# Linear attention and top-1 experts on one core: in three projection tiles the key maximum stands behind the reciprocal, the next tile's statistics behind the query feature, the value sum behind the rows' low part

## Chip, cores and metric

The kernel runs on one core of a Trainium2 chip (trn2). The metric is device time in microseconds of one execution, here the median of 3 runs.

## What is computed

A pre-norm block of two parts over 2048 tokens of width 512, in float32. The first part is linear attention with 32 heads of 16 (a learned feature map of two softmaxes per head); the second sends each token to one of 8 experts (top 1).

```python
def _A_ref(x, wqkv, w_phi, wo):
    H = 32; Dh = D // H
    qkv = (lambda x, *d: x.transpose(*d))((x @ wqkv).reshape(B, S, 3, H, Dh), 2, 0, 3, 1, 4)
    q, k, v = qkv[0], qkv[1], qkv[2]
    pq = jnp.einsum("bhsd,hdf->bhsf", q, w_phi)
    pk = jnp.einsum("bhsd,hdf->bhsf", k, w_phi)
    phi_q = jnp.concatenate([_softmax(pq, axis=-1), _softmax(-pq, axis=-1)], axis=-1)
    phi_k = jnp.concatenate([_softmax(pk, axis=-1), _softmax(-pk, axis=-1)], axis=-1)
    kv = jnp.einsum("bhsf,bhsd->bhfd", phi_k, v)
    z  = jnp.einsum("bhsf->bhf", phi_k)
    num = jnp.einsum("bhqf,bhfd->bhqd", phi_q, kv)
    den = jnp.einsum("bhqf,bhf->bhq", phi_q, z)[..., None] + 1e-6
    ...
h = x + _A_ref(_layernorm(x, axis=-1), A_wqkv, A_w_phi, A_wo)
h2 = h + _B_ref(_layernorm(h, axis=-1), B_w_gate, B_w1, B_w2)
```

## The kernel before

**Stages.** The tokens are cut into 16 tiles of 128 rows (`NT`). A first stage (the projection tiles) walks over them, projects each to keys, values and queries, builds the features and adds up the state. A second stage multiplies the query features by the state, projects out and ranks the experts. The rest runs the experts' two matrices over groups of tokens. Every float32 product is made of three matmuls on a high and a low part (`mm3`, L89): high by high, high by low, low by high, where the first factor is loaded as the weights. The low part is the number less its high part.

**A projection tile c** (the loop at L826). TensorE runs the key projection `pk` of tile c (12 matmuls of 512 columns), the value projection `pv` of tile c+1 (24 of 260 columns, L671), the query projection `pq` of tile c (12 of 512), then the state products `kvps` of tile c-1 (L708) and the 8 transposes `ptq` of the query feature of tile c-1 (L717). In the projections the rows' parts `xh` and `xl` are the weights that are loaded; in a value projection the third matmul is the first to need `xl`.

**The features** (`feat1`, `feat1b`, `feat2`, L643 to L668). VectorE takes minimum `mn` and maximum `mx` of each head from PSUM and writes `t`, the differences to both; ScalarE takes the exponential of `t`, scaled by `rstd`; VectorE sums it (`sm`, L661) and takes the reciprocal (L662); GpSimd (POOL) multiplies, which gives the feature `ph` (L664). In tile c this is done for the query of tile c-1 (`feat2` at L831) and for the key of tile c, then the query of tile c is begun.

**Statistics** (`s_lna`, L612). The mean and variance of the rows of tile c+2: ScalarE's sum (L616), POOL's `xmv` (L617, L620), ScalarE's square (L619), then POOL's `xve` and `rstd` (L622, L623). They are written in tile c and run on into tile c+1. **Values** (`s_v`, `s_ve`, `s_vf`): ScalarE copies `pv` of tile c+1 to `v`, scaled by `rstd` (L682), copies the gate columns `xwg` (L684) and makes `vt` from a row and `rm` = mean times `rstd` (POOL, L693; ScalarE, L697); POOL adds `vt` to `v` (L702). **Rows** (`s_x`, L626): ScalarE rounds the transposed rows of tile c+2 to `xh` (L84 in `hi_of`), POOL writes `xl` (L634). `xh` and `xl` have two buffers and wait for the query projection that reads the old ones.

**What sets the order.** The Tile framework places the instructions of each engine in one row at build time, by the code's order and its own estimates; `with after(i)` (L147) keeps the instructions within it behind `i`. On the chip each instruction waits, by semaphores, for the results and buffers that it needs. `pin` holds the instructions that others are kept behind: `pin["f2"]` is the last feature's multiplication, `pin["rc"]` the last reciprocal, `pin["ex"]` the last exponential.

Of the kernel before, what the change touches and what calls it, by code (L numbers as in the profile page):

```python
# [16 lines left out]
OP = mybir.AluOpType  # L17
AX = mybir.AxisListType
# [31 lines left out]
VC = 4 * (DH + 1)  # L50
KW = 32
LNA = 1


@with_exitstack
def kernel(
# [14 lines left out]
    V, A, G, T = nc.vector, nc.scalar, nc.gpsimd, nc.tensor  # L71
# [73 lines left out]
    pin = {}  # L145

    def after(i):  # L147
        return tc.issue_after(i.ins) if i is not None else ExitStack()
# [266 lines left out]
    with ExitStack() as actx:  # L415
# [40 lines left out]
        st = [dict() for _ in range(NT)]  # L456
# [79 lines left out]
        if True:  # L536
# [75 lines left out]
            def s_lna(c):  # L612
                xt, sm, mv = st[c]["xt"], work.tile([P, 2], F32, name="xsum", bufs=4), work.tile([P, 2], F32, name="xmv", bufs=4)
                jk = wp.tile([P, D], BF16, name="jk", bufs=2)
                with after(pin.get("pq")):
                    A.activation(jk, xt, AF.Copy, accum_out=sm[:, 0:1])  # L616
                G.tensor_scalar(mv[:, 1:2], sm[:, 0:1], -1.0 / D, None, op0=OP.mult)  # L617
                with after(pin["ex"]):
                    st[c]["sq"] = A.activation(jk, xt, AF.Square, bias=mv[:, 1:2], accum_out=sm[:, 1:2])  # L619
                G.tensor_scalar(mv[:, 0:1], sm[:, 0:1], 1.0 / D, None, op0=OP.mult)  # L620
                ve, rstd = work.tile([P, 1], F32, name="xve"), work.tile([P, 1], F32, name="rstd", bufs=4)
                G.tensor_scalar(ve, sm[:, 1:2], 1.0 / D, EPS, op0=OP.mult, op1=OP.add)  # L622
                G.tensor_tensor(rstd, ve, nhalf, op=OP.pow)  # L623
                st[c]["mean"], st[c]["rstd"] = mv[:, 0:1], rstd

            def s_x(c, eng=G):  # L626
                v = st[c]["xT"].rearrange("p (k t) -> p k t", k=KD)
                if c < NT - 1:
                    xh, xl = [work.tile([P, KD, P], F32R, name=n) for n in ("xh", "xl")]
                else:  # L630
                    xh, xl = [wp.tile([P, KD, P], F32R, name=n) for n in ("xhe", "xle")]
                st[c]["xi"] = hi_of(xh, v)
                st[c]["x"] = xh, xl
                return eng.tensor_tensor(xl, v, xh.bitcast(F32), op=OP.subtract)  # L634

            def split_o(t):
                v = slice(0, D // 2)
                r = wo_raw[t // 2][:, t % 2, :].rearrange("p (i d) -> p i d", i=2)
                with after(st[t + 5]["v"]):
                    hi_of(wohi[:, t, :, v], r)  # L640
                return lambda: G.tensor_tensor(wolo[:, t, :, v], r, wohi[:, t, :, v].bitcast(F32), op=OP.subtract)

            def feat1(p, c, whole=True):  # L643
                pv = p.rearrange("p (h f) -> p h f", f=DH)
                mn = work.tile([P, H], F32, name="mn")
                V.tensor_reduce(mn, pv, AX.X, OP.min)
                t = wp.tile([P, H, 2, DH], F32, name="t", bufs=3)
                V.tensor_tensor(t[:, :, 1, :], bc(mn, DH), pv, op=OP.subtract)
                return feat1b(p, c, t) if whole else t

            def feat1b(p, c, t):
                pv = p.rearrange("p (h f) -> p h f", f=DH)
                mx = work.tile([P, H], F32, name="mx")
                V.tensor_reduce(mx, pv, AX.X, OP.max)
                pin["f1"] = V.tensor_tensor(t[:, :, 0, :], pv, bc(mx, DH), op=OP.subtract)  # L655
                pin["ex"] = A.activation(t, t, AF.Exp, scale=st[c]["rstd"])  # L656
                return t.rearrange("p h s f -> p (h s) f")

            def feat2(t, tail=None):
                sm = work.tile([P, 2 * H], F32, name="sm")  # L660
                V.tensor_reduce(sm, t, AX.X, OP.add)  # L661
                pin["rc"] = V.reciprocal(sm, sm)  # L662
                ph = work.tile([P, NB * ROW], F32, name="ph", tag="ph", bufs=3)[:, 0:HF]
                pin["f2"] = G.tensor_tensor(ph.rearrange("p (a f) -> p a f", f=DH), t, bc(sm, DH), op=OP.mult)  # L664
                if tail:
                    with after(pin["f2"]):
                        tail()
                return ph  # L668
# [3 lines left out]
            def s_v(c):  # L672
                with after(pin["pj"]):
                    p, m, pw = proj2(st[c]["x"], wvhi, wvlo, "pv")
                s_ve(c, p, pw)
                s_vf(c)
                return m

            def s_ve(c, p, pw=None):
                v = v17[c % 3].rearrange("p (i h) f -> p i h f", i=2)[:, :, :, 0:DH]  # L680
# [10 lines left out]
            def s_vf(c, eng=None):  # L691
                rm = work.tile([P, 1], F32, name="rm")
                G.tensor_tensor(rm, st[c]["mean"], st[c]["rstd"], op=OP.mult)  # L693
                vt, v = row("vt", 2, "pc"), v17[c % 3][:, :, 0:DH]
                if eng is None:
                    with after(st[c]["v"] if c < 5 else None):
                        A.activation(vt, csv, AF.Copy, scale=rm)  # L697
                else:
                    eng.tensor_scalar(vt, csv, rm, None, op0=OP.mult)
                def add():  # L700
                    with after(pin["f2"]):
                        G.tensor_tensor(v, v, vt.rearrange("p (h f) -> p h f", f=DH), op=OP.add)  # L702

                if c > 1:
                    add()
                return add

# [51 lines left out]
            with after(warmup(6)):  # L759
                pc = bank("pcs")  # L760
                m = T.matmul(pc[:, 0:E], onesf, gsum, start=True, stop=True)
# [21 lines left out]
            with after(m):  # L783
                p0, m, _ = proj2(st[0]["x"], wvhi, wvlo, "pv", True)
# [41 lines left out]
            for c in range(NT - 1):  # L826
# [2 lines left out]
                    s_qt(0)  # L829
                if 0 < c < NT - 2:  # L830
                    st[c - 1]["fq"] = feat2(st[c - 1]["tq"])  # L831
                lo_o = split_o(c - 5) if 5 <= c < 9 else None
                tk = feat1(pk, c)
                if c == 0:
                    pf = [bank("pf") if dt < 2 else pss.tile([P, 512], F32, name="pf", tag="s") for dt in range(KD)]
                    for dt in range(KD):
                        fold_half(wq_raw, pf[dt], dt, 0)
                        fold_half(wq_raw, pf[dt], dt, 1)
                        fold_split(pf[dt], dt, wqhi, wqlo)
                    kvps.append(pss.tile([P, NG, 64], F32, name="kvps", tag="s")[:, :, 0:(DH + 1) * KW // 32])  # L840
                elif c < NT - 2:
                    vm = s_v(c + 1)
                if c in (3, 4):
                    pg = bank("pog")
                    fold_gate(pg, 2 * c - 6)
# [16 lines left out]
                else:  # L862
# [11 lines left out]
                        pq = proj(st[c]["x"], wqhi, wqlo, "pq")  # L874
                    if c + 2 < NT - 1:
                        with after(pin["f2"] if c == 1 else None):
                            s_x(c + 2)
                    st[c]["fk"] = feat2(tk, lo_o)
                    if c < NT - 3:
                        st[c]["tq"] = feat1(pq, c)  # L880
# [793 lines left out]
```

## Time and profile before

| | us |
|---|---|
| median of 3 runs (lowest to highest) | 633.94 (633.76 to 634.34) |
| the profiled execution | 633.68 |
| its span, from the first to the last instruction | 632.0 |
| TensorE busy in the span | 622.7 |

The profile is of one execution. Its time is 1.7 us longer than its span, for what lies around the first and last instruction. Busy times are of instructions on an engine; two that follow each other on one engine overlap by up to 0.1 us. Projection tile 8 begins at 98.85 us, tile 11 ends at 140.22 us.

### The profile page before, as it was taken

Reading aid. Unit: us, or ns where it says so; the run is one execution under the profiler, and the core shown is the slowest. Engines: PE = TensorE matmul, PEld = TensorE weight load, DVE = VectorE, ACT = ScalarE, POOL = GpSimd, SP = SyncE. Lnnn points to the kernel's source line nnn. Section 1 sums busy time; section 2 is a strip of 40 time slices with the busy share of each in tenths; the row PEclk is TensorE's granted clock in tenths of the full one; section 3 lists DMA queues with packets and bytes.
Section 4 is the critical chain, followed back from the end, with each engine's and each line's share of the span. In section 5 each row is a group of like instructions: output and inputs, shape, how many; then the busy total and the mean of one; then the engine's idle time right before and its main releaser. Section 6 shows DMA issues by size and latency. Waiting matters only on the chain. (4 is left out here: it accounts for less than half of the span.)

```text
span 632.0 us, 14731 instructions
## 1 busy us (share of the span) xinstructions
PE 622.7 (99%) x5455; PEld 555.6 (88%) x5455; DVE 452.8 (72%) x900; ACT 373.5 (59%) x673; POOL 247.5 (39%) x345
## 2 busy tenths in 40 slices
PE   9999999999999999999999999999999999999996
PEld 8888888888889999868998898989999889988884
DVE  7988786888898789965325666666556775579992
ACT  6666767577434439634325666566456666668781
POOL 5586788787616555621122221120301420023120
PEclk9999999999999999999999999999999999999999
DMA  8712111111002359249121485563755585569921
GB/s 319 250 36 66 37 51 52 51 52 35 18 20 85 118 204 380 100 158 419 48 69 52 164 307 204 199 235 135 272 170 208 186 335 164 195 222 374 415 81 36
DMA packets 25689, 103.09 MB, mean 163 GB/s; under 512 B 3422, under 2 KB 3422, under 8 KB 17536
## 3 DMA queue, kind: packets, MB, share of 16 engines
q1 hardware_dynamic: 21088, 88.15, 39.1%
q0 software_dynamic: 4368, 13.82, 6.5%
q8 instruction: 46, 0.75, 0.5%
q14 instruction: 43, 0.35, 0.2%
q10 hardware_dynamic: 144, 0.02, 0.0%
HBM read 93.56 MB, written 8.81 MB: 162 GB/s over the span
## 5 line engine op out<-in xcount | busy, mean ns | idle before, releaser
L235 DVE TENSOR_TENSOR wlo<-raw,whi 128x1024 fp32r<-128x1024 f32 (+1 forms) x133 | 151.9, 1165 | 27.3 <-ACT whi L84 25.6
L84 ACT ACTIVATE whi<-raw 128x1024 fp32r<-128x1024 f32 (+1 forms) x134 | 129.3, 998 | 1.6 <-DVE wlo L235 0.6
L168 POOL DMA_INDIRECT xg<-hbuf,gidx x34 | 42.9, 1261 | 132.6 <-DMA out_dram<-xg,sidx 33.3
L87 DVE TENSOR_TENSOR hA<-hs,hA 128x256 fp32r<-128x256 f32 (+1 forms) x84 | 36.6, 436 | 74.9 <-ACT hA L84 53.9
L664 POOL TENSOR_TENSOR ph<-t,sm 128x1024 f32<-128x1024 f32 x32 | 62.1, 1942 | 16.8 <-DVE sm L662 16.5
L90 PE MATMUL gw<-xhi,whi 128*128 128x256 f32 x224 | 64.1, 286 | 0.0
L92 PE MATMUL gw<-xhi,wlo 128*128 128x256 f32 x224 | 63.0, 281 | 0.0
L91 PE MATMUL gw<-xlo,whi 128*128 128x256 f32 x224 | 63.0, 281 | 0.0
L1423 ACT ACTIVATE hs<-gw 128x256 f32<-128x256 f32 x56 | 21.4, 383 | 63.2 <-PE gw L92 52.8
L661 DVE TENSOR_REDUCE sm<-t 128x64 f32<-128x1024 f32 x32 | 38.9, 1215 | 20.0 <-ACT t L656 17.9
L656 ACT ACTIVATE t<-t,rstd 128x1024 f32<-128x1024 f32 x32 | 36.8, 1151 | 27.2 <-DVE t L655 24.7
L181 POOL DMA_INDIRECT out_dram<-xg,sidx x17 | 19.9, 1169 | 79.4 <-DVE xg L1275 44.1
L90 PEld LDWEIGHTS gw<-xhi,whi 128*128 128x128 f32 x224 | 42.2, 188 | 1.7
L91 PEld LDWEIGHTS gw<-xlo,whi 128*128 128x128 f32 x224 | 42.3, 189 | 1.6
L92 PEld LDWEIGHTS gw<-xhi,wlo 128*128 128x128 f32 x224 | 42.2, 188 | 0.0
L90 PE MATMUL po<-wohi,xh 128*128 128x260 f32 x128 | 37.4, 293 | 0.0
L84 ACT ACTIVATE hA<-hs 128x256 fp32r<-128x256 f32 (+1 forms) x84 | 35.8, 427 | 2.6
L92 PE MATMUL po<-wohi,xl 128*128 128x260 f32 x128 | 36.5, 286 | 0.1
L91 PE MATMUL po<-wolo,xh 128*128 128x260 f32 x128 | 36.1, 282 | 0.0
L90 PE MATMUL pv<-wvhi,xh 128*128 128x260 f32 x120 | 34.3, 286 | 0.0
L92 PE MATMUL pv<-wvhi,xl 128*128 128x260 f32 x120 | 33.9, 283 | 0.0
L91 PE MATMUL pv<-wvlo,xh 128*128 128x260 f32 x120 | 33.9, 282 | 0.0
(425 smaller groups left out, 1922.9 us busy)
## 6 DMA issues: line engine op xcount, KB each, us to landing
raw<-in_w_dram SPq DMA_DIRECT2D x63, 1024.0 KB, 5.8
xt<-in_x_dram SPq DMA_DIRECT2D x32, 256.0 KB, 2.7
hbuf<-hb SPq DMA_DIRECT2D x8, 515.0 KB, 3.5
xT<-in_xTs_dram SPq DMA_DIRECT2D x16, 256.0 KB, 2.7
phT<-in_wv_dram SPq DMA_DIRECT2D x4, 256.0 KB, 3.6
phT<-in_wqkT_dram SPq DMA_DIRECT2D x4, 256.0 KB, 5.3
phT<-in_wqkT_dram SPq DMA_DIRECT2D x2, 512.0 KB, 6.1
phT<-in_wo_dram SPq DMA_DIRECT2D x2, 512.0 KB, 7.7
```

Source lines behind the costliest of these rows:

```text
L84: return A.activation(dst, src, AF.Copy)
L87: return V.tensor_tensor(dst, src, hi.bitcast(F32), op=OP.subtract)
L90: T.matmul(ps, ahi, bhi, start=first, stop=False)
L91: T.matmul(ps, ahi, blo, start=False, stop=False)
L92: return T.matmul(ps, alo, bhi, start=False, stop=last)
L168: G.indirect_dma_start(out=dst[0:n, :], out_offset=None, in_=hbuf if col else hbuf[0:S // 2, :], in_offset=bass.IndirectOffsetOnAxis(ap=gi ...
L181: m = G.indirect_dma_start(out=out, out_offset=bass.IndirectOffsetOnAxis(ap=sidx[0:n, col:col + 1], axis=0), in_=src[0:n, 0:D], in_offset= ...
L235: return eng.tensor_tensor(lo, r, h.bitcast(F32), op=OP.subtract)
L656: pin["ex"] = A.activation(t, t, AF.Exp, scale=st[c]["rstd"])
L661: V.tensor_reduce(sm, t, AX.X, OP.add)
L664: pin["f2"] = G.tensor_tensor(ph.rearrange("p (a f) -> p a f", f=DH), t, bc(sm, DH), op=OP.mult)
L1423: A.activation(h, p, AF.Silu)
```

## The change

In the tiles of `GL` (c = 8, 9, 10) three things are placed elsewhere; what is computed is the same. The key's maximum `mx` is kept behind the reciprocal of the query's sums (`pin["rc"]`). The last steps of the statistics of tile c+1, `xve` and `rstd`, are a function of their own (`s_lnb`) and kept behind the query feature's multiplication (`pin["f2"]`). The value sum (`add`) is kept behind `xl` of tile c+2.

```diff
--- before.py
+++ after.py
@@ -50,6 +50,7 @@
 VC = 4 * (DH + 1)
 KW = 32
 LNA = 1
+GL = range(8, 11)
 
 
 @with_exitstack
@@ -618,6 +619,12 @@
                 with after(pin["ex"]):
                     st[c]["sq"] = A.activation(jk, xt, AF.Square, bias=mv[:, 1:2], accum_out=sm[:, 1:2])
                 G.tensor_scalar(mv[:, 0:1], sm[:, 0:1], 1.0 / D, None, op0=OP.mult)
+                st[c]["ms"] = mv, sm
+                if c - 1 not in GL:
+                    s_lnb(c)
+
+            def s_lnb(c):
+                mv, sm = st[c]["ms"]
                 ve, rstd = work.tile([P, 1], F32, name="xve"), work.tile([P, 1], F32, name="rstd", bufs=4)
                 G.tensor_scalar(ve, sm[:, 1:2], 1.0 / D, EPS, op0=OP.mult, op1=OP.add)
                 G.tensor_tensor(rstd, ve, nhalf, op=OP.pow)
@@ -640,18 +647,19 @@
                     hi_of(wohi[:, t, :, v], r)
                 return lambda: G.tensor_tensor(wolo[:, t, :, v], r, wohi[:, t, :, v].bitcast(F32), op=OP.subtract)
 
-            def feat1(p, c, whole=True):
+            def feat1(p, c, whole=True, behind=None):
                 pv = p.rearrange("p (h f) -> p h f", f=DH)
                 mn = work.tile([P, H], F32, name="mn")
                 V.tensor_reduce(mn, pv, AX.X, OP.min)
                 t = wp.tile([P, H, 2, DH], F32, name="t", bufs=3)
                 V.tensor_tensor(t[:, :, 1, :], bc(mn, DH), pv, op=OP.subtract)
-                return feat1b(p, c, t) if whole else t
-
-            def feat1b(p, c, t):
+                return feat1b(p, c, t, behind) if whole else t
+
+            def feat1b(p, c, t, behind=None):
                 pv = p.rearrange("p (h f) -> p h f", f=DH)
                 mx = work.tile([P, H], F32, name="mx")
-                V.tensor_reduce(mx, pv, AX.X, OP.max)
+                with after(behind):
+                    V.tensor_reduce(mx, pv, AX.X, OP.max)
                 pin["f1"] = V.tensor_tensor(t[:, :, 0, :], pv, bc(mx, DH), op=OP.subtract)
                 pin["ex"] = A.activation(t, t, AF.Exp, scale=st[c]["rstd"])
                 return t.rearrange("p h s f -> p (h s) f")
@@ -673,8 +681,7 @@
                 with after(pin["pj"]):
                     p, m, pw = proj2(st[c]["x"], wvhi, wvlo, "pv")
                 s_ve(c, p, pw)
-                s_vf(c)
-                return m
+                return m, s_vf(c)
 
             def s_ve(c, p, pw=None):
                 v = v17[c % 3].rearrange("p (i h) f -> p i h f", i=2)[:, :, :, 0:DH]
@@ -697,11 +704,11 @@
                         A.activation(vt, csv, AF.Copy, scale=rm)
                 else:
                     eng.tensor_scalar(vt, csv, rm, None, op0=OP.mult)
-                def add():
-                    with after(pin["f2"]):
+                def add(behind=None):
+                    with after(pin["f2"]), after(behind):
                         G.tensor_tensor(v, v, vt.rearrange("p (h f) -> p h f", f=DH), op=OP.add)
 
-                if c > 1:
+                if c > 1 and c - 1 not in GL:
                     add()
                 return add
 
@@ -829,8 +836,11 @@
                     s_qt(0)
                 if 0 < c < NT - 2:
                     st[c - 1]["fq"] = feat2(st[c - 1]["tq"])
+                    if c in GL:
+                        with after(pin["f2"]):
+                            s_lnb(c + 1)
                 lo_o = split_o(c - 5) if 5 <= c < 9 else None
-                tk = feat1(pk, c)
+                tk = feat1(pk, c, True, pin["rc"] if c in GL else None)
                 if c == 0:
                     pf = [bank("pf") if dt < 2 else pss.tile([P, 512], F32, name="pf", tag="s") for dt in range(KD)]
                     for dt in range(KD):
@@ -839,7 +849,7 @@
                         fold_split(pf[dt], dt, wqhi, wqlo)
                     kvps.append(pss.tile([P, NG, 64], F32, name="kvps", tag="s")[:, :, 0:(DH + 1) * KW // 32])
                 elif c < NT - 2:
-                    vm = s_v(c + 1)
+                    vm, add = s_v(c + 1)
                 if c in (3, 4):
                     pg = bank("pog")
                     fold_gate(pg, 2 * c - 6)
@@ -874,7 +884,9 @@
                         pq = proj(st[c]["x"], wqhi, wqlo, "pq")
                     if c + 2 < NT - 1:
                         with after(pin["f2"] if c == 1 else None):
-                            s_x(c + 2)
+                            lx = s_x(c + 2)
+                        if c in GL:
+                            add(lx)
                     st[c]["fk"] = feat2(tk, lo_o)
                     if c < NT - 3:
                         st[c]["tq"] = feat1(pq, c)
```

In the rows below the numbers in the names are those of buffers; line numbers after the change are those of the changed file. On POOL, tile 8, before: the statistics of tile 9 (`xmv_1615`, `xve`, `rstd`), then `rm`, then the feature of tile 7's query (`ph_1641`), the value sum of tile 9 and the low part `xl` of tile 10's rows.

```order
L617 TENSOR_SCALAR xmv_1615<-xsum_1614 128x1
L620 TENSOR_SCALAR xmv_1615<-xsum_1614 128x1
L622 TENSOR_SCALAR xve_1621<-xsum_1614 128x1
L623 TENSOR_TENSOR rstd_1622<-xve_1621,fixed_66 128x1
L693 TENSOR_TENSOR rm_1679<-xmv_1615,rstd_1622 128x1
L664 TENSOR_TENSOR ph_1641<-t_1564,sm_1638 128x1024
L702 TENSOR_TENSOR v17_0_201<-v17_0_201,vt_1681 128x32x16
L634 TENSOR_TENSOR xl_1702<-xT_1537,xh_1701 128x512
```

The same place after:

```order
L618 TENSOR_SCALAR xmv_1615<-xsum_1614 128x1
L621 TENSOR_SCALAR xmv_1615<-xsum_1614 128x1
L672 TENSOR_TENSOR ph_1637<-t_1564,sm_1634 128x1024
L629 TENSOR_SCALAR xve_1639<-xsum_1614 128x1
L630 TENSOR_TENSOR rstd_1640<-xve_1639,fixed_66 128x1
L700 TENSOR_TENSOR rm_1679<-xmv_1615,rstd_1640 128x1
L641 TENSOR_TENSOR xl_1701<-xT_1537,xh_1700 128x512
L709 TENSOR_TENSOR v17_0_201<-v17_0_201,vt_1681 128x32x16
```

The query feature has moved ahead of `xve`, `rstd` and `rm`, and `xl` ahead of the value sum.

On ScalarE, tile 8, before: the statistics' square, `vt`, `v` and `xwg` of tile 9, the exponential of tile 8's key (`t_1646`), the high part `xh` of tile 10's rows.

```order
L619 ACTIVATE jk_1616,xsum_1614<-xt_1386,xmv_1615 128x512
L697 ACTIVATE vt_1681<-csv_204,rm_1679 128x512
L682 ACTIVATE v17_0_201<-pv_1652,rstd_1622 128x32x16
L684 ACTIVATE xwg_170<-pv_1652 128x8
L656 ACTIVATE t_1646<-t_1646,rstd_1473 128x1024
L84 ACTIVATE xh_1701<-xT_1537 128x512
```

And after:

```order
L620 ACTIVATE jk_1616,xsum_1614<-xt_1386,xmv_1615 128x512
L689 ACTIVATE v17_0_201<-pv_1652,rstd_1640 128x32x16
L664 ACTIVATE t_1646<-t_1646,rstd_1473 128x1024
L691 ACTIVATE xwg_170<-pv_1652 128x8
L704 ACTIVATE vt_1681<-csv_204,rm_1679 128x512
L85 ACTIVATE xh_1700<-xT_1537 128x512
```

`vt` has moved from ahead of `v` to behind the exponential and `xwg`; `v` now stands directly behind the square. `xh` is still behind all four.

On VectorE, tile 8, before: sum and reciprocal of tile 7's query (`sm_1638`), maximum and difference of tile 8's key, then the sum of the key's exponentials and the query of tile 8.

```order
L661 TENSOR_REDUCE sm_1638<-t_1564 128x64
L654 TENSOR_REDUCE mx_1648<-pk_1625 128x32
L662 RECIPROCAL sm_1638<-sm_1638 128x64
L655 TENSOR_TENSOR t_1646<-pk_1625,mx_1648 128x32x16
L661 TENSOR_REDUCE sm_1705<-t_1646 128x64
L646 TENSOR_REDUCE mn_1711<-pq_1688 128x32
```

And after:

```order
L669 TENSOR_REDUCE sm_1634<-t_1564 128x64
L670 RECIPROCAL sm_1634<-sm_1634 128x64
L662 TENSOR_REDUCE mx_1648<-pk_1621 128x32
L663 TENSOR_TENSOR t_1646<-pk_1621,mx_1648 128x32x16
L653 TENSOR_REDUCE mn_1711<-pq_1687 128x32
L669 TENSOR_REDUCE sm_1705<-t_1646 128x64
```

The reciprocal has moved ahead of the key's maximum, and the minimum of the query ahead of the sum of the key's exponentials. TensorE's row is the same before and after.

## Rows read from the trace of the kernel before

**Rows 1.** The page's span and first part: busy time, share of the span and number of instructions of each engine.

```profile
span 632.0 us, 14731 instructions
PE 622.7 (99%) x5455; PEld 555.6 (88%) x5455; DVE 452.8 (72%) x900; ACT 373.5 (59%) x673; POOL 247.5 (39%) x345
```

**Rows 2.** Whom TensorE waited for over the whole span: line waited at, releaser, us in total, times, longest us. The longest three.

```profile
PE warm L751 <- DVE onesf L419: 1.3, 1, 1.3
PE mh L90 <- PEq L1577: 0.6, 1, 0.6
PE ptq L722 <- POOL ph L664: 0.3, 1, 0.3
...
```

**Rows 3.** Windows of the projection tiles 8, 9, 10 and 11, each from the first matmul of its key projection `pk` to that of the next tile. Columns: window, its length, then busy us (and instructions) of PE, PEld, DVE, ACT and POOL, the granted clock, DMA share, GB/s.

```profile
98.85:109.37 10.52, 10.20 (x124) 8.79 (x121) 8.30 (x13) 6.65 (x14) 8.68 (x10) 1.00 0.16 50
109.37:119.71 10.34, 10.22 (x123) 8.80 (x122) 8.11 (x13) 6.46 (x14) 8.88 (x11) 1.00 0.17 55
119.71:130.07 10.36, 10.23 (x124) 8.81 (x122) 8.71 (x13) 6.59 (x14) 7.62 (x10) 1.00 0.16 51
130.07:140.22 10.15, 10.15 (x124) 8.80 (x122) 8.50 (x14) 6.48 (x13) 7.96 (x11) 1.00 0.19 53
```

**Rows 4.** TensorE's timeline from the end of tile 8's value projection on: start us, length us, instruction, and in brackets the idle time before it with its releaser. `pv<-wvhi,xl` at 112.49, 122.83 and 133.18 is the third matmul of the value projection in tiles 9, 10 and 11; `kvps` are the state products and `ptq` the query transposes at a tile's end (tiles 8 to 12).

```profile
104.48 0.28 PE L92 MATMUL pv<-wvhi,xl 128*128 128x260 f32 x1
...
107.46 0.74 PE L713 MATMUL kvps<-v,ph 128*32 128x17 f32 x64
...
108.52 1.09 PE L722 MATMUL ptq<-ident,ph 128*128 128x128 f32 x8 [0.33 <-POOL ph L664]
...
109.37 0.48 PE L90 MATMUL pk<-wkhi,xh 128*128 128x512 f32 x1
...
109.69 0.39 PE L91 MATMUL pk<-wklo,xh 128*128 128x512 f32 x1
...
112.49 0.28 PE L92 MATMUL pv<-wvhi,xl 128*128 128x260 f32 x1
...
118.86 1.09 PE L722 MATMUL ptq<-ident,ph 128*128 128x128 f32 x8
...
122.83 0.28 PE L92 MATMUL pv<-wvhi,xl 128*128 128x260 f32 x1
...
133.18 0.28 PE L92 MATMUL pv<-wvhi,xl 128*128 128x260 f32 x1
...
139.37 1.09 PE L722 MATMUL ptq<-ident,ph 128*128 128x128 f32 x8
...
149.52 1.09 PE L722 MATMUL ptq<-ident,ph 128*128 128x128 f32 x8
```

**Rows 5.** POOL's timeline in tile 8 and the start of tile 9, same columns.

```profile
105.34 0.19 POOL L622 TENSOR_SCALAR xve<-xsum 128x1 f32<-128x1 f32 x1 [0.76 <-ACT jk L619]
...
105.62 0.58 POOL L623 TENSOR_TENSOR rstd<-xve,fixed 128x1 f32<-128x1 f32 x1
...
106.27 0.19 POOL L693 TENSOR_TENSOR rm<-xmv,rstd 128x1 f32<-128x1 f32 x1
...
106.52 1.94 POOL L664 TENSOR_TENSOR ph<-t,sm 128x1024 f32<-128x1024 f32 x1
...
108.42 1.20 POOL L702 TENSOR_TENSOR v<-v,vt 128x512 f32<-128x512 f32 x1
...
109.58 1.29 POOL L634 TENSOR_TENSOR xl<-xT,xh 128x512 fp32r<-128x512 f32 x1
...
111.36 1.94 POOL L664 TENSOR_TENSOR ph<-t,sm 128x1024 f32<-128x1024 f32 x1 [0.49 <-DVE sm L662]
...
113.26 1.31 POOL L641 TENSOR_TENSOR wolo<-phT,wohi 128x512 fp32r<-128x512 f32 x1
...
114.52 0.25 POOL L617 TENSOR_SCALAR xmv<-xsum 128x1 f32<-128x1 f32 x1
```

**Rows 6.** ScalarE's timeline in tile 8, same columns.

```profile
104.45 0.72 ACT L619 ACTIVATE jk<-xt,xmv 128x512 bf16<-128x512 f32 x1 [0.46 <-POOL xmv L617]
...
106.50 0.73 ACT L697 ACTIVATE vt<-csv,rm 128x512 f32<-128x512 f32 x1 [1.24 <-POOL rm L693]
...
107.13 0.67 ACT L682 ACTIVATE v<-pv,rstd 128x512 f32<-128x512 f32 x1
...
107.70 0.16 ACT L684 ACTIVATE xwg<-pv 128x8 f32<-128x8 f32 x1
...
107.76 1.15 ACT L656 ACTIVATE t<-t,rstd 128x1024 f32<-128x1024 f32 x1
...
108.80 0.62 ACT L84 ACTIVATE xh<-xT 128x512 fp32r<-128x512 f32 x1
```

**Rows 7.** VectorE's timeline in tile 8, same columns; the last row is the sum over tile 8's key exponentials.

```profile
104.11 1.21 DVE L661 TENSOR_REDUCE sm<-t 128x64 f32<-128x1024 f32 x1
...
105.24 0.68 DVE L654 TENSOR_REDUCE mx<-pk 128x32 f32<-128x512 f32 x1
...
105.83 0.55 DVE L662 RECIPROCAL sm<-sm 128x64 f32<-128x64 f32 x1
...
106.29 0.63 DVE L655 TENSOR_TENSOR t<-pk,mx 128x512 f32<-128x512 f32 x1
...
109.01 1.22 DVE L661 TENSOR_REDUCE sm<-t 128x64 f32<-128x1024 f32 x1 [2.08 <-ACT t L656]
```

## The prediction

> **What bounds the kernel now.** I read the page's first part, then whom TensorE waited for, then each projection tile's window, and last the engines' timelines at the tiles that the change touches. TensorE is busy for 622.7 of 632.0 us [rows 1]; all its listed waits for other engines come to a few microseconds, the longest 1.3 us at the start [rows 2]. So TensorE sets the time, and a microsecond that it waits in the projection stage is not given back: after the stage nothing is listed that it waits for longer than 0.6 us.
>
> Tiles 8, 9 and 10 (the three of the new range) take 10.52, 10.34 and 10.36 us from key projection to key projection, tile 11 takes 10.15 and TensorE is busy in all of it [rows 3]. The difference, 0.37 + 0.19 + 0.21 = 0.77 us, is TensorE waiting at the end of each tile for the query feature: the transposes into `ptq` start 0.05 us after the feature `ph` is written on POOL (106.52 + 1.94 = 108.46, transposes at 108.52) [rows 4, 5]. [...]
>
> **What the change can win.** The reciprocal is taken ahead of the key maximum. The sum of the query's exponentials ends at 104.11 + 1.21 = 105.32; with 0.04 allowed for the hand-over the reciprocal starts at 105.36, where it now stands at 105.83 behind the 0.68 us maximum [rows 7]. It then ends at 105.91, and POOL takes `ph` at 105.98, for 106.52 now, provided that the statistics of the next tile (ending at 106.27 + 0.19 = 106.46) no longer stand ahead of it [rows 5]. `ph` would end at 107.92, and the state products ahead of the transposes run until 107.46 + 0.74 = 108.20 [rows 4]. So the wait is gone in tile 8; the most that all three tiles can win is the 0.77 us. Moving the maximum costs nothing on TensorE: its exponential is then ready at 107.17 and waits for ScalarE anyway.
>
> **What it moves onto a path.** `xve`, `rstd` and `rm` now stand behind the 1.94 us `ph` on POOL. ScalarE's row holds, in the new order, the square of the statistics, then `v` (scaled by `rstd` of the next tile), then the exponential of the keys, `xwg`, `vt`, and only then `xh`, the high part of the rows two tiles on. POOL's low part `xl` waits for `xh`, and the value projection of the next tile waits for `xl` in its third matmul. Tile 8, with the durations of rows 5 and 6, POOL's steps overlapping by 0.04 and ScalarE's by 0.10 as there, a POOL step that needs another engine's or its own last result 0.08 behind it (`rm` stands 0.07 behind `rstd`), and ScalarE 0.03 behind POOL (`vt` stands 0.04 behind `rm`):
> - POOL: `xve` at 107.88, `rstd` 108.16 to 108.74, `rm` to 109.00 (now 105.34, 105.62, 106.46).
> - ScalarE: `v` at 108.77 for 0.67 (now 107.13), exponential of the keys 109.33 to 110.48 (now 107.76 to 108.91), `xwg` 0.16, `vt` 0.73, `xh` 111.07 to 111.69 (now from 108.80).
> - POOL: `xl` 111.77 to 113.06 (now 109.58 to 110.87).
> - TensorE: the third value matmul stands at 112.49 now [rows 4], and 0.37 earlier, at 112.12, once the wait for `ph` is gone. It starts 0.05 after `xl`, at 113.11: a new wait of 0.99 us. Before, `xl` had been done for 1.6 us.
>
> So tile 8 ends up 0.62 us behind. Does it run off in tile 9? The sum over the key exponential starts 0.10 behind it [rows 6, 7], at 110.58, the query's exponential follows at 114.16, while POOL does `xl`, the value sum (1.20, to 114.22), the key feature (to 116.12), the output weight's low part (1.31, to 117.39), two small steps, and the query feature from 117.72 to 119.66. The transposes, due at 119.29 (118.86, less the 0.19 waited now, plus 0.62), start at 119.71: 0.42 us. From there the same steps as in tile 8 put `rstd` at 120.47, `v` at 120.50, `xh` at 122.80 and `xl` at 124.79. TensorE's third value matmul of that round, 122.83 now, comes 0.62 + 0.42 - 0.19 = 0.85 late, at 123.68, and starts at 124.84: 1.16 us. I carry the same arithmetic on:
> - Tile 10: no wait at the transposes (the 0.21 of now is saved), the sum of the query's exponentials ends at 128.38, the reciprocal at 128.96, `ph` runs 129.04 to 130.98, `rstd` until 131.78, `v` at 131.81, `xl` until 136.13. The third value matmul, 133.18 now, comes 0.85 + 1.16 - 0.21 = 1.80 late, at 134.98, and starts at 136.18: 1.20 us.
> - Tile 11 is in the old order, but POOL is behind: value sum until 137.28, key feature until 139.17, two small steps, ScalarE's square until 140.20, statistics until 141.40, query feature 141.36 to 143.30. The transposes, 139.37 now, are due 3.00 later, at 142.37, and start at 143.35: 0.98 us.
> - Tile 12: `ph` until 153.70, transposes (149.52 now) due 3.98 later, at 153.50, and starting at 153.75: 0.25 us. From tile 13 on every feature is done before its use again.
>
> Sum: -0.77 + (0.99 + 1.16 + 1.20) + (0.42 + 0.98 + 0.25) = 4.2 us. The same arithmetic on the order of before gives TensorE's starts of tiles 9 to 12 back within 0.1 us, so I take 0.3 us as the error of the sum if the mechanism holds. The profiled run took 633.68 us, 0.26 below the median of 633.94; 633.68 + 4.2 = 637.9, and against the median 638.1.
>
> Two prices have no row. A wait between two matmuls of one accumulation is not in the trace; the nearest rows are the transposes' start 0.05 behind `ph`, and the first key matmul after them, which takes 0.48 where its neighbour takes 0.39 [rows 4, 5]. Bounds for each of three: 0.05, which the sum holds, and 0.05 + 0.09; so 0 to +0.3. And the new place of the value sum, behind `xl`: nothing on TensorE, since its state products come a tile later (kept from -0.1 to 0.1).
>
> [...] ScalarE's row of now shows a ready instruction standing behind a waiting one: the value projection of tile 8 ends at 104.48 + 0.28 = 104.76, `v` reads it only at 107.13, behind `vt`, which had idled 1.24 us for `rm` [rows 4, 6]. If ScalarE could take the exponential or `xh` ahead of the waiting `v`, the second and third bullets of tile 8 fall and the sum is -0.8; held to its order, it is +4.2. [...]
>
> **The rivals.**
> - In time (the other side): `xl` comes early enough, and the change does what it saves: 633.94 - 0.8 = 633.2 us, 0.13% faster, which is within the 0.2% that a measurement of this kernel can tell from no change. For it `xl` of tile 8 would have to end by 112.07, 1.0 us ahead of my 113.06. Against it: only the 0.67 of `v` or the 1.15 of the exponential, taken out of the row ahead of `xh`, is that large. Chance 0.07.
> - Caught up: the three waits for `xl` come, but POOL has recovered by tiles 11 and 12, so that 0.98 and 0.25 fall away: +3.0, 636.9 us. It needs `ph` of tile 11 a microsecond earlier; POOL is busy for 7.96 of tile 11's 10.15 us [rows 3], so it has room, but not ahead of that `ph`. Chance 0.12.
> - Not caught up: each new wait restarts TensorE dearer than 0.05, and tiles 12 and 13 wait as long as 11 does: +4.2 + 0.3 + 1.0, 639.4 us. Chance 0.08.
> - The clock falls: four waits of about a microsecond within 40 us. [...] The longest wait here, 1.3 us at the start, leaves the mean at 0.999 of full speed and every window at 1.00. [...] Chance 0.03.
> - The forecast: 638.1 us, by itself 637.4 to 638.8. Chance 0.70.
>
> **How the numbers follow.** Range 636.4 to 639.6 us: it holds the forecast, "caught up" with its error, and "not caught up", 0.9 less some tail. Slower by over 0.2% (1.27 us): all but the first, 0.91 after rounding for what I have not seen; within 0.2%: 0.07; faster by over 0.2%: 0.02, since no row holds more than 0.77 us to win.
>
> **What would show it.** In the profile after: TensorE's list of waits gains `pv` waiting for POOL's `xl`, three times about 1 us, and `ptq` for `ph` with the longest near 1 us in tile 11; tiles 9, 10 and 11 (key projection to key projection) become some 11.5, 11.3 and 12.3 us long and tile 8 10.1; ScalarE's `v` waits for `rstd` in three tiles, 2 to 4 us of idle each; in tile 8 the query feature starts 0.5 us earlier. If `xl` in tile 8 ends before 112.1, the forecast is wrong at its root; if it ends near 113 and TensorE's time is not 1 us longer, something later gives it back that I have not found.

## The result and the profile after

The changed kernel takes 639.15 us (median of 6 runs, 638.6 to 639.4), the kernel before 633.85 us (6 runs, 633.1 to 634.34): a ratio of 1.0082 with a 95% interval of 1.0071 to 1.0093, 5.3 us slower. Forecast were 638.1 us and a range of 636.4 to 639.6.

The page's span and first part of the changed kernel, the answer to [rows 1]:

```profile
span 637.7 us, 14731 instructions
PE 624.8 (98%) x5455; PEld 555.3 (87%) x5455; DVE 453.4 (71%) x900; ACT 373.0 (58%) x673; POOL 245.6 (39%) x345
```

The span grew by 5.7 us with the same number of instructions, and no engine but TensorE is busier by more than 0.6 us. TensorE's own 2.1 us more lie for the most part in tiles 9 to 11 below, where matmuls around a wait are recorded longer (the third value matmul with 0.39 us, for 0.28 in [rows 4]); so the time is waiting. Whom TensorE waited for (us in total, times, longest), the answer to [rows 2]:

```profile
PE pv L93 <- POOL xl L641: 2.5, 3, 0.8
PE warm L758 <- DVE onesf L420: 1.3, 1, 1.3
PE ptq L729 <- POOL ph L672: 1.3, 3, 0.9
...
PE mtr L198 <- ACT hs L191: 0.4, 1, 0.4
```

New at the top are three waits of the value projection for `xl`, and `ptq` waits 1.3 us in place of 0.3. The windows of tiles 8 to 12, from key projection to key projection, columns as in [rows 3]:

```profile
99.37:109.50 10.13, 10.13 (x123) 8.79 (x122) 8.81 (x13) 3.77 (x9) 7.55 (x8) 1.00 0.18 53
109.50:121.23 11.73, 10.68 (x123) 8.77 (x122) 8.41 (x12) 6.47 (x12) 8.76 (x10) 1.00 0.15 47
121.23:132.79 11.56, 10.72 (x123) 8.76 (x122) 8.41 (x12) 6.47 (x12) 7.59 (x10) 1.00 0.15 47
132.79:145.23 12.44, 10.74 (x124) 8.77 (x122) 7.79 (x12) 9.23 (x17) 8.68 (x12) 1.00 0.14 43
145.23:155.67 10.44, 10.20 (x123) 8.78 (x122) 8.80 (x13) 6.67 (x14) 7.62 (x10) 1.00 0.08 27
```

The five tiles take 56.30 us; before, they took 51.53 (tile 12, not shown there, took 10.15). That is 4.77 of the 5.7 us of span. The rest: tile 8 begins 0.53 later than in the profile of before, and about 0.4 is lost behind tile 13, as much as the `mtr` wait of the list. I count neither as the change's: in all kernels here but the last below POOL, ScalarE and VectorE run the order of before in every tile ahead of 8, and the profiles of the experiments below begin that tile anywhere between 98.75 and 99.74; and none of them shows that `mtr` wait for `hs`. The granted clock was 1.00 in all five tiles.

TensorE's timeline from tile 8's end on (columns as in [rows 4]; `ptq` is the end of tiles 8, 9, 11 and 12, the `pv` rows of one tile stand together):

```profile
108.66 1.09 PE L729 MATMUL ptq<-ident,ph 128*128 128x128 f32 x8
109.50 0.48 PE L91 MATMUL pk<-wkhi,xh 128*128 128x512 f32 x1
...
112.47 0.39 PE L91 MATMUL pv<-wvhi,xh 128*128 128x260 f32 x1
112.70 0.28 PE L92 MATMUL pv<-wvlo,xh 128*128 128x260 f32 x1
113.82 0.39 PE L93 MATMUL pv<-wvhi,xl 128*128 128x260 f32 x1 [0.84 <-POOL xl L641]
114.05 0.28 PE L91 MATMUL pv<-wvhi,xh 128*128 128x260 f32 x1
114.17 0.28 PE L92 MATMUL pv<-wvlo,xh 128*128 128x260 f32 x1
...
120.39 1.09 PE L729 MATMUL ptq<-ident,ph 128*128 128x128 f32 x8 [0.21 <-POOL ph L672]
...
125.62 0.39 PE L93 MATMUL pv<-wvhi,xl 128*128 128x260 f32 x1 [0.84 <-POOL xl L641]
...
137.17 0.39 PE L93 MATMUL pv<-wvhi,xl 128*128 128x260 f32 x1 [0.84 <-POOL xl L641]
...
144.38 1.09 PE L729 MATMUL ptq<-ident,ph 128*128 128x128 f32 x8 [0.85 <-POOL ph L672]
...
154.82 1.09 PE L729 MATMUL ptq<-ident,ph 128*128 128x128 f32 x8 [0.24 <-POOL ph L672]
```

The wait of tile 8's `ptq` is gone. In tile 9 the third value matmul starts 4.32 us behind the key projection (113.82 - 109.50), where it started 3.12 behind it (112.49 - 109.37 in [rows 4]). It is 1.20 late, though only 0.84 is shown as idle. Part of that is lost ahead of it: the first value matmul starts 2.97 us behind the key projection for 2.88 before, 0.06 behind the end of a late `xh`, and the second follows it 0.23 behind, in place of 0.12, so that 0.20 is gone before `xl` is needed. The third then comes 1.00 later than it would behind the second: a row of a value matmul lasts 0.28 while the next one starts 0.12 behind it when nothing holds it (114.05 and 114.17), and the idle time shown runs only from the end of the row ahead (112.70 + 0.28 = 112.98, to 113.82). (Rows on TensorE thus overlap by 0.16, more than the 0.1 us named ahead of the prediction for all engines.) And the fourth follows the third 0.23 behind it, in place of 0.12. **What a wait costs is read from starts, not from the idle column.**

POOL's timeline in tile 8 and the start of tile 9, the answer to [rows 5]:

```profile
106.60 1.93 POOL L672 TENSOR_TENSOR ph<-t,sm 128x1024 f32<-128x1024 f32 x1 [1.50 <-DVE sm L670]
108.61 0.19 POOL L629 TENSOR_SCALAR xve<-xsum 128x1 f32<-128x1 f32 x1
108.89 0.57 POOL L630 TENSOR_TENSOR rstd<-xve,fixed 128x1 f32<-128x1 f32 x1
...
112.50 1.27 POOL L641 TENSOR_TENSOR xl<-xT,xh 128x512 fp32r<-128x512 f32 x1 [2.77 <-ACT xh L85]
```

ScalarE's, the answer to [rows 6], with the waits of `v` in the two tiles that follow:

```profile
109.50 0.69 ACT L689 ACTIVATE v<-pv,rstd 128x512 f32<-128x512 f32 x1 [3.72 <-POOL rstd L630]
110.08 1.14 ACT L664 ACTIVATE t<-t,rstd 128x1024 f32<-128x1024 f32 x1
...
111.79 0.62 ACT L85 ACTIVATE xh<-xT 128x512 fp32r<-128x512 f32 x1
...
121.30 0.69 ACT L689 ACTIVATE v<-pv,rstd 128x512 f32<-128x512 f32 x1 [2.19 <-POOL rstd L630]
...
132.85 0.69 ACT L689 ACTIVATE v<-pv,rstd 128x512 f32<-128x512 f32 x1 [3.18 <-POOL rstd L630]
```

And VectorE's, the answer to [rows 7]:

```profile
105.87 0.55 DVE L670 RECIPROCAL sm<-sm 128x64 f32<-128x64 f32 x1
...
107.00 0.69 DVE L663 TENSOR_TENSOR t<-pk,mx 128x512 f32<-128x512 f32 x1
...
111.32 1.22 DVE L669 TENSOR_REDUCE sm<-t 128x64 f32<-128x1024 f32 x1 [2.53 <-ACT xwg L691]
```

The ring is to be seen row by row: `ph` ends at 108.53, `rstd` at 109.46, `v` starts at 109.50 behind 3.72 us of idle ScalarE, although the differences for the key's exponential, next in its row, were written at 107.69; `xh` ends at 112.41 (the first value matmul of tile 9 starts at 112.47), `xl` runs from 112.50 to 113.77, and TensorE goes on at 113.82.

### The profile page after: what moved, and what is told of

The parts are those of the page before. It is cut to its first block, busy times and chain, and to the rows that moved or that the text cites. A ratio compares the mean times of both kernels' runs of the same rounds, so it can differ in the third digit from the quotient of the medians.

```text
span 637.7 us, 14731 instructions
## 1 busy us (share of the span) xinstructions
PE 624.8 (98%) x5455; PEld 555.3 (87%) x5455; DVE 453.4 (71%) x900; ACT 373.0 (58%) x673; POOL 245.6 (39%) x345
```

## The experiments

The theory: ScalarE's `v`, waiting for a `rstd` that is now late, holds the exponential and `xh` in its row; that makes `xl`, and through it TensorE, late. The rivals: the loss comes from POOL's new row by itself (the statistics behind the feature, or the value sum behind `xl`); from the moved maximum; or it comes once, and a longer range doesn't repeat it. In the sums below, tiles 8 to 12 of before took 51.53 us. Diffs are against the changed kernel.

| kernel | median, us | before beside it | ratio (95%) | tiles 8 to 12, against before |
|---|---|---|---|---|
| `v` behind `xh` | 632.8 | 633.67 | 0.9984 (0.9975 to 0.9993) | -0.85 |
| `v` behind the exponential | 634.44 | 633.59 | 1.0014 (1.0004 to 1.0023) | +0.75 |
| maximum alone | 633.22 | 633.67 | 0.9989 (0.9979 to 0.9999) | -0.61 |
| maximum and value sum | 633.4 | 633.67 | 0.9995 (0.9986 to 1.0004) | -0.57 |
| value sum alone | 633.91 | 633.59 | 1.0005 (0.9995 to 1.0014) | +0.52 |
| statistics alone | 635.14 | 633.67 | 1.0018 (1.0009 to 1.0028) | +1.26 |
| whole change, tile 8 only | 637.07 | 633.59 | 1.0054 (1.0038 to 1.0071) | +4.10 |
| whole change, tiles 5 to 10 | 642.88 | 633.59 | 1.0145 (1.0128 to 1.0161) | +8.74 (tiles 5 to 12) |

**`v` behind `xh`, all three moves kept.** ScalarE's `v`, `xwg` and `vt` are made behind `xh` of the same tile:

```diff
-                s_ve(c, p, pw)
+                if c - 1 in GL:
+                    return m, lambda: (s_ve(c, p, pw), s_vf(c))[1]
+                s_ve(c, p, pw)
                 return m, s_vf(c)
...
                         if c in GL:
+                            with after(st[c + 2]["xi"]), after(pin["ex"]):
+                                add = add()
                             add(lx)
```

> All three moves kept; on ScalarE alone, in tiles 8 to 10, `v`, `xwg` and `vt` are placed behind `xh`, and `v` behind the key's exponential. POOL's and VectorE's rows stay as in the change. My theory (a waiting `v` holds the exponential and `xh` behind it on ScalarE): no wait for `xl`, `xh` of tile 8 starts near 108.8 us again, the transposes' waits go too; tiles 8, 9, 10 each 10.15 us; 633.2 us, 0.1% faster than before. Rival (POOL's row by itself, with the statistics and the value sum behind the features, is what comes late): `xl` still late, at least 636 us.

Measured: 632.8 us. ScalarE in tile 8, and the window of tile 9, of this kernel:

```profile
107.22 1.15 ACT L664 ACTIVATE t<-t,rstd 128x1024 f32<-128x1024 f32 x1 [1.95 <-DVE t L663]
108.28 0.61 ACT L85 ACTIVATE xh<-xT 128x512 fp32r<-128x512 f32 x1
109.00 0.69 ACT L691 ACTIVATE v<-pv,rstd 128x512 f32<-128x512 f32 x1
```

```profile
109.00:119.14 10.14, 10.14 (x123) 8.78 (x122) 8.69 (x13) 7.37 (x15) 9.59 (x12) 1.00 0.20 54
```

`rstd` is as late as in the changed kernel (108.39 here, with tile 8 beginning 0.50 earlier), but the exponential and `xh` no longer stand behind `v`, and ScalarE idles only 0.11 us for it (108.89 to 109.00). `xh` starts at 108.28 for 111.79, TensorE is busy through the whole tile, and all five tiles take 10.13 or 10.14. The whole loss was ScalarE's row: the rows of POOL and VectorE hold the same instructions in the same order as in the changed kernel, from tile 8 to tile 12, and the rivals that blame them by themselves fall. This version is faster than both kernels; than the kernel before by 0.16%, with a 95% interval of 0.07 to 0.25%.

**`v` behind the exponential, but ahead of `xh`.** Half of the same:

```diff
-                s_ve(c, p, pw)
-                return m, s_vf(c)
+                with after(pin["ex"] if c - 1 in GL else None):
+                    s_ve(c, p, pw)
+                    return m, s_vf(c)
```

> All three moves are kept, and on ScalarE v, xwg and vt stand behind the key's exponential in tiles 8 to 10, but still ahead of xh (half of what the version with xh ahead of v does). Theory: v still waits for rstd, but only xh is held behind it; xh and xl come about 1.0 us earlier in tile 8, where the third value matmul has its wait of 0.84 us: that wait falls to nothing in tile 8, to 0.1 to 0.2 in tile 9, and the transposes wait 0.2 to 0.3 us in tiles 9, 11 and 12; tiles 8 to 12 together 0.2 us longer than before, 633.9 us. Rival (xh alone behind v makes the loss, the exponential does not count): 637 us or more.

Measured: 634.44 us, tiles 10.13, 10.73, 10.49, 10.48 and 10.45. TensorE's rows in tile 9 of this kernel:

```profile
112.12 0.28 PE L92 MATMUL pv<-wvlo,xh 128*128 128x260 f32 x1
112.42 0.39 PE L93 MATMUL pv<-wvhi,xl 128*128 128x260 f32 x1
...
119.00 1.09 PE L730 MATMUL ptq<-ident,ph 128*128 128x128 f32 x8 [0.23 <-POOL ph L672]
```

With the exponential ahead of `v`, 4.0 of the 4.77 us are gone, and with `xh` ahead of `v` too, as in the version above, another 1.6; the rival (637 or more) falls. The exponential's place does two things at once: `xh` starts 11.36 us into tile 8 in place of 12.42, and the key feature is begun earlier. How the 4.0 are shared between them is not shown. The expected +0.2 us was too small by half a microsecond. The third value matmul still starts 0.30 behind the second, for the usual 0.12, and the next follows at 112.64, 0.22 on: 0.28 lost, with no idle time shown. Such hidden pieces in tiles 9 and 10 were left out of the expectation.

**Statistics back in their old place.** The maximum and the value sum stay moved:

```diff
-                if c - 1 not in GL:
-                    s_lnb(c)
+                s_lnb(c)
...
-                    if c in GL:
-                        with after(pin["f2"]):
-                            s_lnb(c + 1)
```

> The statistics stand ahead of the query feature again; the key maximum stays behind the reciprocal and the value sum behind `xl`. My theory: `v` finds `rstd` ready, no wait for `xl`; 633.5 us (one transposes' wait of 0.2 us left in tile 8). Rival (the value sum's or the maximum's move costs): 635 us or more.

Measured: 633.4 us. Tiles 10.34, 10.20, 10.15, 10.13 and 10.14, no wait for `xl`. Without the statistics' move there is no loss.

**Statistics alone.** The maximum and the value sum go back:

```diff
-                tk = feat1(pk, c, True, pin["rc"] if c in GL else None)
+                tk = feat1(pk, c)
...
-                if c > 1 and c - 1 not in GL:
+                if c > 1:
                     add()
...
-                        if c in GL:
-                            add(lx)
```

> Only the statistics are moved behind the query feature; maximum and value sum stand as before. In this build ScalarE's row has `v` behind the key's exponential, not ahead of it. My theory: the exponential is not held, but `xh` still stands behind `v` and `vt`; one wait for `xl` of about 0.8 us in tile 9 and one of 0.3 us in tile 11, 634.6 us. Rival (late statistics alone are the whole cost, whatever stands behind `v`): 638 us or more. Second rival (late statistics cost nothing by themselves): 633.9 us.

Measured: 635.14 us, so +1.5: neither the whole 5 nor nothing, and 0.5 more than expected. ScalarE's `v` and `xh` in tile 8, POOL's value sum and `xl`, and the two waits of TensorE for `xl`, of this kernel:

```profile
110.01 0.69 ACT L689 ACTIVATE v<-pv,rstd 128x512 f32<-128x512 f32 x1 [1.34 <-POOL rstd L630]
...
111.27 0.63 ACT L85 ACTIVATE xh<-xT 128x512 fp32r<-128x512 f32 x1
```

```profile
111.46 1.21 POOL L709 TENSOR_TENSOR v<-v,vt 128x512 f32<-128x512 f32 x1 [1.21 <-ACT vt L704]
112.62 1.28 POOL L641 TENSOR_TENSOR xl<-xT,xh 128x512 fp32r<-128x512 f32 x1
```

```profile
113.95 0.39 PE L93 MATMUL pv<-wvhi,xl 128*128 128x260 f32 x1 [0.72 <-POOL xl L641]
...
134.85 0.39 PE L93 MATMUL pv<-wvhi,xl 128*128 128x260 f32 x1 [0.20 <-POOL xl L641]
```

With the maximum in its old place the framework put `v` behind the key's exponential (107.52 in this kernel), so on ScalarE only `xh` is held. On POOL `xl` is held once more: the value sum, still ahead of it here, waits for `vt`, so that `xl` starts 0.72 us behind the end of `xh` (111.90), for 0.09 in the changed kernel. Late statistics thus reach `xl` through either row. The parts don't add up: +1.26 for the statistics and -0.57 for the other two make +0.7, not +4.77. What is missing is the framework's own answer to the combination, `v` ahead of the exponential, which no line of the diff says. With `v` put behind the exponential by hand, all three moves together cost +0.75 (above), close to the sum of the parts. Which of the other two moves makes the framework put `v` ahead is not shown.

**Maximum alone.** Statistics and value sum as before (both edits of the statistics' return, and the last two of the one above):

> Only the key's maximum is moved behind the reciprocal. My theory: it wins part of the transposes' 0.77 us and costs nothing: 633.4 us, tiles 9 and 10 at 10.15 us. Rival (the later maximum delays the key's exponential and so the loop): 634.5 us or more.

Measured: 633.22 us, tiles 10.36, 10.15, 10.13, 10.14 and 10.14. Most of what there was to win (0.77 us by the forecast) comes from this part by itself, and tile 8 keeps a `ptq` wait of 0.16.

**Value sum alone.** Statistics and maximum as before (both edits of the statistics' return, and the first of the statistics alone):

> Of the three moves only the value sum is made, behind the rows' low part, in tiles 8 to 10. Theory (the waiting v on ScalarE makes the loss; the value sum moves no v): no third value matmul waits for the low part; the sum now stands 1.2 us later on POOL, so that the key feature and then a query feature come a little later: transposes' waits of about 0.2, 0.7 and 0.2 us, tiles 8 to 12 together 0.5 us longer than in the kernel before, 634.4 us. Rival (the value sum's new place is what holds the state products or the low part back, and makes the bulk of the loss): 636 us or more, with TensorE waiting in kvps or in pv.

Measured: 633.91 us, tiles 10.53, 10.80, 10.44, 10.13 and 10.15. Its longest wait, in tile 9 (TensorE's timeline):

```profile
120.12 1.09 PE L728 MATMUL ptq<-ident,ph 128*128 128x128 f32 x8 [0.58 <-POOL ph L671]
```

The 0.5 us is where it was expected, at the transposes, and no matmul waits for `xl`. In time it can't be told from before.

**The whole change in tile 8 alone.**

```diff
-GL = range(8, 11)
+GL = range(8, 9)
```

> The whole change in tile 8 alone. Theory: one new wait in tile 9's third value matmul, 0.8 to 0.9 us, and then one run-off at the transposes of tile 9, which is in the old order with POOL late, 2.2 to 2.5 us, and 0.2 in tile 10: tiles 8 to 12 together 2.8 us longer than before, 636.7 us. Rival (each changed tile costs its own third of the loss, with nothing run off later): +1.6 us, 635.4 us.

Measured: 637.07 us, the median of four runs that fall into two pairs (637.55 and 637.97 us with a mean granted clock of 0.995 and 0.996, and 636.31 and 636.58 with 0.999 and 0.998). The profile is of the first. TensorE in tile 9, then windows around tile 9's end (columns as in [rows 3]), of this kernel:

```profile
113.17 0.39 PE L93 MATMUL pv<-wvhi,xl 128*128 128x260 f32 x1 [0.84 <-POOL xl L641]
...
118.79 0.74 PE L720 MATMUL kvps<-v,ph 128*32 128x17 f32 x64
121.61 1.97 PE L729 MATMUL ptq<-ident,ph 128*128 128x128 f32 x8 [2.08 <-POOL ph L672]
```

```profile
121.00:121.60 0.60, 0.00 (x0) 0.00 (x0) 0.00 (x0) 0.60 (x2) 0.60 (x2) 0.84 0.00 0
121.60:124.50 2.90, 2.89 (x11) 2.70 (x12) 2.30 (x4) 2.50 (x5) 2.37 (x2) 0.50 0.03 6
124.50:125.00 0.50, 0.50 (x3) 0.36 (x3) 0.50 (x2) 0.32 (x2) 0.44 (x1) 0.67 0.06 20
```

One wait for `xl`, then a run-off of 2.08 us, since tile 9 in the old order has the statistics ahead of its query feature on POOL: as the theory had it, and the rival of a third per tile (635.4) falls. The two runs with the higher mean clock, 636.31 and 636.58, lie close to the expected 636.7; the 0.2 expected at tile 10's transposes is not there. What was not expected is the clock: TensorE stood idle from 119.53 to 121.61, the granted clock fell in that stretch (0.84 from 121.00 to 121.60) and was 0.50 for some 3 us behind it. The eight transposes took 1.97 us for 1.09. If TensorE's work keeps pace with the granted clock, 2.9 us at 0.50 lose about 1.5 us: an estimate from the window above. The five tiles of this profile are 1.3 us longer than expected (+4.10 for +2.8), and 1.3 us is what parts the two pairs of runs.

**The whole change in six tiles.** `GL = range(5, 11)`.

> The whole change in tiles 5 to 10, six in place of three. Theory: each changed tile behind the first is paced by the ring POOL statistics, ScalarE v, exponential, xh, POOL xl, and takes about 11.7 us in place of 10.1 to 10.4, so three more tiles cost 1.5 to 1.6 us each, and the run-off in the two tiles behind stays as it is, about 2.5 us: tiles 5 to 12 together 8.5 us longer than before, 642.3 us. Rival (a loss once, which a longer range does not repeat): 639 us. Second rival (the waits grow from tile to tile): 645 us or more.

Measured: 642.88 us. Windows of tiles 7, 9 and 11 of this kernel:

```profile
90.14:101.95 11.81, 10.73 (x123) 8.77 (x122) 8.41 (x12) 6.99 (x13) 8.80 (x11) 1.00 0.15 46
...
113.78:125.59 11.81, 10.73 (x123) 8.76 (x122) 8.41 (x12) 6.47 (x12) 8.80 (x11) 1.00 0.16 48
...
137.15:149.58 12.43, 10.73 (x123) 8.76 (x122) 7.78 (x12) 9.23 (x17) 8.67 (x12) 1.00 0.17 44
```

The ring settles at 11.82 us a round in tiles 7 to 9, tile 10 takes 11.56 as in the changed kernel, and the run-off in tile 11 is as there too (12.43 for 12.44). Both rivals (639 and 645 us) fall: once the waits have begun, the loss is per tile and doesn't grow. The first of the six changed tiles makes none to speak of: tile 6 takes 10.64, and no wait for `xl` is shown in it. In tile 5 ScalarE's `v`, waiting for `rstd`, starts 9.02 us into the tile (78.38 - 69.36), in tile 8 of the changed kernel 10.13 (109.50 - 99.37), and what stands behind it is that much earlier: `xh` starts 11.32 us into the tile (80.68) for 12.42. So six changed tiles make five waits. The five waits, one a tile and 4.2 us together, left the granted clock at 1.00 in every window from tile 5 to tile 12.

## Why the prediction was right

The mechanism held in every step; the size was 0.5 us short of the traced 4.77, more than the 0.3 that the forecast gave as the error of its sum. The measured 639.15 us lies in the stated range, but above the 637.4 to 638.8 that the forecast by itself allowed. Lateness is taken from starts: without waits a tile's third value matmul starts 3.12 us and its `ptq` 9.30 us behind its key projection (118.86 - 109.37 - 0.19 by [rows 4] and the forecast's wait), and a tile takes 10.13.

- **The gain** was put at 0.77; against tiles of 10.13 it is 0.84 (0.40 + 0.21 + 0.23), and 0.04 more in tiles 11 and 12. Tile 8 took the 10.1 that was forecast. In tiles 9 and 10 the transposes' wait went with the maximum's move, as the maximum alone shows; in tile 8, where that version takes 10.36, it needed the statistics behind the feature as well.
- **The value matmuls' waits** were put at 0.99, 1.16 and 1.20. The starts of 113.82, 125.62 and 137.17 are 1.20, 1.27 and 1.26 late: 3.73 for 3.35. The step that was mis-sized is the hand-over on POOL and VectorE. Less the 0.53 that tile 8 began later, the reciprocal stands at 105.34 (forecast 105.36), but `ph` at 106.07 (105.98): 0.18 behind the reciprocal's end, not the 0.07 taken (rows below). `xve` starts at 108.08 (107.88), 0.08 behind the end of `ph` and not overlapping it by 0.04. From there `v`, the exponential, `xh` and `xl` are each 0.19 to 0.22 behind their forecast times, and their distances to one another are as forecast.
- **The restart** in the middle of an accumulation, which had no row, was bounded at 0 to +0.3 and taken as 0. It measured 0.11 for each of the three (the fourth matmul 0.23 behind the third for 0.12): +0.33, a little above the bound. This is the other half of the miss. That the first value matmul would wait for `xh`, too, is not in the forecast; it adds nothing, since the third waits for longer.
- **The transposes' waits** were put at 0.42, 0, 0.98 and 0.25. By starts they are 0.28, 0.03, 0.92 and 0.29: 1.52 for 1.65. TensorE, later by the two terms above, waits a little less for the same `ph`.
- **The sum:** -0.88 + 3.73 + 0.33 + 1.52 = 4.70, 0.07 short of the 4.77. Against the medians, 5.3 us were measured; the forecast was 4.2. The 0.5 between the medians and the five tiles has no place in this sum; in the table above medians and tiles differ by up to 0.6 either way.

The forecast's 0.07 is what the key's feature takes: in the kernel before it starts 0.08 or 0.09 behind its reciprocal (111.36 in [rows 5], with the reciprocal's end at 111.28). The query's feature takes longer, and rows of before had it: wherever POOL waits for it there in tiles 5 to 12, it starts 0.14 or 0.15 behind. The reciprocal and the feature in tile 11, of the kernel before:

```profile
136.31 0.55 DVE L662 RECIPROCAL sm<-sm 128x64 f32<-128x64 f32 x1
```

```profile
137.00 1.94 POOL L664 TENSOR_TENSOR ph<-t,sm 128x1024 f32<-128x1024 f32 x1 [0.63 <-DVE sm L662]
```

The row from which the forecast took ScalarE's order was misread in one point: `v` needs `rstd` besides the value projection, and that was written only at 106.20 [rows 5], so `v` was not ready at 104.76. `xwg` was, which reads the projection alone; it ran at 107.70, behind `v` and behind the 1.24 us that ScalarE idled ahead of `vt` [rows 6], and shows the same order.

Of the rivals, **in time** needed `xl` in tile 8 a microsecond sooner, and said that only the 0.67 of `v` or the exponential out of the way of `xh` was that large; the version with both ahead of `v` (-0.85 us) has `xl` in time, and the one with the exponential alone (+0.75 us) nearly. **Caught up** fell with tile 11's 12.44. **Not caught up** (639.4) lies nearest to the measured time and had half its reason right, the dearer restart; its other half, tiles 12 and 13 waiting as long as 11 does, is not there (tile 12 takes 10.44). **The clock falls** did not happen in the changed kernel (1.00 in all five windows). It did in the version with tile 8 alone: 0.50 behind a wait of 2.08 us, and there its price was some 1.3 us by the tiles, 1.5 by the estimate from the clock.

That the order of ScalarE's row holds what stands behind a waiting instruction is shown twice: by the changed kernel, where the exponential, ready at 107.69, starts at 110.08 behind `v` while ScalarE idles, and by the version with `v` behind `xh`: same rows on POOL and VectorE, other row on ScalarE, no loss.

## What to carry to other kernels

When a small step is put behind a large one on one engine, look up who waits for its result, and above all what is queued behind that waiter on its engine: here 1.9 us on POOL were harmless in themselves and cost 5 us through a row of ScalarE that held work which needed nothing from them. If a producer is made late, its consumer has to move back in its row as well; a framework that orders by its own estimates may even move it forward, so read the order as built. And a change in one tile can cost more than its share of a change in three (2.9 of 5.3 us here in the two runs with the higher clock, 3.5 by the median of all four), because the tile behind it, in the old order, pays the run-off.

## What was not expected of the hardware

- A single idle stretch of TensorE of 2.08 us, with one of 0.84 some 8 us ahead of it, was followed by a granted clock of 0.50 for about 3 us in the profiled execution (tile 8 alone); the mean clock was 0.995 and 0.996 in two executions of four, 0.999 and 0.998 in the others. Waits of 4.2 us together, one a tile in five tiles in a row, left it at 1.00 (the whole change in tiles 5 to 10).
- A wait between matmuls of one accumulation cost more than its idle time: where 0.84 is shown, the matmul came 1.00 later behind the one ahead than without a wait (113.82 for 112.82), and the next one 0.11 later still; a delay of 0.18 (112.42 for 112.24 with `v` behind the exponential) showed no idle at all.
- Hand-overs differed by more than was taken for one figure: `rstd` to `v` 0.04 us (109.46 to 109.50), `xl` to TensorE 0.05 (113.77 to 113.82), POOL's `xve` 0.08 behind the end of `ph` (108.53 to 108.61), where the value sum behind `ph` in the kernel before overlaps it by 0.04 (108.46 and 108.42); the reciprocal to `ph`, wherever POOL waits for it in tiles 5 to 12 of the kernel before and the changed one, 0.08 to 0.09 for the key, 0.14 to 0.18 for the query. Why the last two differ is not shown.
